# Longer DMA runs for one K cache of a two-part decode attention: A's K in runs of 16 KB in place of 8 KB

## The chip, the cores and the metric

The kernel runs on one core of a Trainium2 chip. The metric is the device time of one execution in microseconds (us). For each execution two numbers are known: that time, and the span, which is the stretch from the first to the last instruction that the hardware profiler recorded. This text calls their difference the time outside the span. A program on one core has no second die to compare with, so an execution counts as slow if it is over 1.5% above the fastest of its kernel. One run of the kernel before, of some thirty, took 248.25 us; it counts as fast by that rule, and it raises the mean and widens the intervals of its batch (r5 to r8).

## The reference, cut to what matters

Two independent attentions of one query token (A and B), each with 32 query heads over 16 KV heads of 128 dimensions, and a cache of 8192 tokens. A looks at the last 2048 tokens only, B at all of them. The two outputs are concatenated.

```python
q = (x @ wq).reshape(B, Sq, Hq, Dh)              # 576 -> 32 heads of 128
k = repeat(k_cache[:, :, Sk - W:, :], 2)         # A: W = 2048; B: all 8192 tokens
v = repeat(v_cache[:, :, Sk - W:, :], 2)
p = softmax(q @ k.T * Dh ** -0.5)
out = (p @ v).reshape(B, Sq, Hq * Dh) @ wo       # 4096 -> 576
```

Nearly everything is reading. In bf16 B's K and V are 67.1 MB, A's K and V 8.4 MB each, and the two wq and wo together 18.9 MB, 102.76 MB in all, each byte used once.

## The kernel before

There are five groups: group 0 is all of A, groups 1 to 4 are four KV heads of B each. A group's K goes to two slots of 4 MB (s = 0, 1), its V to one region of 8 MB. TensorE transposes K in 8 units per group, ScalarE (ACT) and VectorE (DVE) evict the transposed tiles from PSUM to `kt`, TensorE makes the scores, and then come exp, a transpose of the weights, and the product with V. SyncE issues every big load, as soon as its slot is free. The program is written for one instruction stream of TensorE that is looped over the groups, so all groups must have the same shapes there.

```python
def load_k(g, s):
    dst = slots[:, koff(s):koff(s) + SLOT]                 # [128, 16384] bf16
    def go(sp):
        if g:                                              # B: one copy of 4 MB, runs of 32 KB
            i = 4 * (g - 1) + 2 * s
            return sp.dma_start(dst, ks[1][0, i:i + 2, :, :].rearrange("e (p t) d -> p e (t d)", t=128))
        for m in range(4):                                 # A: four copies of 1 MB, runs of 8 KB
            i = 4 * m + 2 * s
            src = ks[0][0, i:i + 2, SK - W_A:, :].rearrange("e (p t) d -> p e (t d)", t=32)
            ins = sp.dma_start(dst[:, m * UNIT:(m + 1) * UNIT], src)
            ...                                            # cut: semaphore counts
        return ins
    ...
def q_stage(g, s):                                         # POOL puts q columns where they pick a head
    def go(pool):
        for e in range(2):
            dst = bass.AP(tensor=qst, offset=s * 264 + e * 130 + 4 * s, ap=[[528, 128], [40, 4], [1, 2]])
            ...
            ins = pool.tensor_copy(dst, src)
    ...
def k_transpose(g, u, place):                              # unit u: 4 x 8 transposes, 4 evictions
    ...
        dst = kt[:, u % NKT, q * 1024:(q + 1) * 1024]
        # q even: ACT copies ktps_bf[q] to dst; q odd: DVE does
```

A run here is one contiguous piece of HBM that lands in one SBUF partition; each is one DMA packet of its size (in r4 below, 6656 more runs are 6656 more packets). With 2048 tokens of 256 bytes and 64 partitions per head, A's run is 32 tokens or 8 KB.

Of the kernel before, what the change touches and what calls it, by code (L numbers as in the profile page):

```python
# [4 lines left out]
BF16 = mybir.dt.bfloat16  # L5
F32 = mybir.dt.float32
# [269 lines left out]
def bass_concat_heads__sliding_block_cached__gqa_block_cached__decode_kernel(  # L276
# [25 lines left out]


    prog = Program(nc)
    add = prog.add
# [8 lines left out]
    pickB = nc.alloc_sbuf_tensor("pickB", [128, 4, 32], F32)  # L314
    same = nc.alloc_sbuf_tensor("same", [128, 128], F32)
    sameB = nc.alloc_sbuf_tensor("sameB", [128, 128], F32)
    selq = nc.alloc_sbuf_tensor("selq", [128, 4, 2], BF16)
    onesf = nc.alloc_sbuf_tensor("onesf", [128, 4], F32)
    qst = nc.alloc_sbuf_tensor("qst", [128, 2 * 264], BF16)
    qcol = nc.alloc_sbuf_tensor("qcol", [128, 2, HQ], BF16)  # L320
# [48 lines left out]
    def setup(pool):  # L369
        for t in (ident, xpad, selq, warm, identf, same, pick, qst):  # L370
            pool.memset(t[:], 0.0)
        pool.memset(onesf[:], 1.0)
        return pool.memset(opj[:], 0.0)

    add("pool", setup, writes=["ident", ("xpad", 0), ("xpad", 1), "selq", "ones", "warm", "identf", "pick", "same",
                               ("qst", 0), ("qst", 1), ("opj", 0), ("opj", 1)])

# [5 lines left out]
    add("pool", select(selq[:], 0, [[-32, 4], [-1, 2]], 1), reads=["selq"], writes=["selq"])  # L383
    for dj in range(-3, 4):
        add("pool", select(same[:], 32 * dj, [[-1, 128]], 1), reads=["same"], writes=["same"])
    add("pool", select(identf[:], 0, [[-1, 128]], 1), reads=["identf"], writes=["identf"])
    for j in range(4):
        add("pool", select(pick[:], -128 * j, [[1, 4], [-1, 128]], 4), reads=["pick"], writes=["pick"])

    def sums(out, view, reads, writes, tag=None):  # L390
        add("dve", lambda dve: dve.tensor_reduce(out, view, AX.X, ALU.add), reads=reads, writes=writes, tag=tag)

# [8 lines left out]
    def load_k(g, s):  # L401
        dst = slots[:, koff(s):koff(s) + SLOT]

        def go(sp):
            if g:
                i = 4 * (g - 1) + 2 * s
                return sp.dma_start(dst, ks[1][0, i:i + 2, :, :].rearrange("e (p t) d -> p e (t d)", t=128))
            for m in range(4):
                i = 4 * m + 2 * s
                src = ks[0][0, i:i + 2, SK - W_A:, :].rearrange("e (p t) d -> p e (t d)", t=32)  # L410
                ins = sp.dma_start(dst[:, m * UNIT:(m + 1) * UNIT], src)
                if m < 3:
                    op.also.append((16, ins))
            return ins
        op = add("sp", go, writes=KS[s], dma="k%d" % s, inc=64)
# [59 lines left out]


    def q_stage(g, s):
        P = min(g, 1)

        def go(pool):  # L480
            for e in range(2):
                dst = bass.AP(tensor=qst, offset=s * 264 + e * 130 + 4 * s, ap=[[528, 128], [40, 4], [1, 2]])
                o = 4 * s + 2 * e + (8 * (g - 1) if P else 0)
                src = bass.AP(tensor=qcol, offset=P * HQ + o, ap=[[2 * HQ, 128], [0 if P else 8, 4], [1, 2]])
                ins = pool.tensor_copy(dst, src)  # L485
            return ins
        add("pool", go, reads=[("qcol", P)], writes=[("qst", s)], tag="q%d" % s)

    def k_transpose(g, u, place):
        s, m = divmod(u, 4)  # L490
        for q in range(4):
            def tr(pe, q=q):
                for t in range(8):
                    o = koff(s) + (32 * m + 8 * q + t) * 128
                    ins = pe.matmul(ktps_bf[q][:, t * 128:(t + 1) * 128], lhsT=slots[:, o:o + 128],  # L495
                                    rhs=ident[:, :], start=True, stop=True, is_transpose=True)
                return ins
            add("pe", tr, reads=KS[s] + ["ident"], writes=[("bank", q)], loop=(g, place + q / 8, None))
            dst = kt[:, u % NKT, q * 1024:(q + 1) * 1024]
            if q % 2 == 0:  # L500
                add("act", lambda act, q=q, dst=dst: act.activation(dst, ktps_bf[q], ACT.Copy),  # L501
                    reads=[("bank", q)], writes=[("kt", u % NKT, q)], tag="e%d%d" % (u, q))
            else:
                add("dve", lambda dve, q=q, dst=dst: dve.tensor_copy(dst, ktps_bf[q]),  # L504
                    reads=[("bank", q)], writes=[("kt", u % NKT, q)], tag="e%d%d" % (u, q))


    def k_scores(g, u, place):
        s, m = divmod(u, 4)

        def mm(pe):
            for e in range(2):
                for j in range(4):
                    rhs = kt[:, u % NKT, j * 1024:(j + 1) * 1024].rearrange("d (x g) -> d x g", g=2)[:, :, e]
                    o = s * 264 + e * 128 + m * 32
                    ins = pe.matmul(sacc[32 * j:32 * j + 32, :], lhsT=qst[:, o:o + 32], rhs=rhs,  # L516
                                    start=(u == 0 and e == 0), stop=True, skip_group_check=True)
            return ins
        add("pe", mm, reads=[("qst", s)] + [("kt", u % NKT, q) for q in range(4)], writes=[B_S],
            loop=(g, place, None))  # L520
# [7 lines left out]
    def softmax_exp(g):  # L528
# [6 lines left out]
        def go(act):  # L535
            src = bass.AP(tensor=sacc, offset=0, ap=[[512, 128], [2, 256], [1, 2], [0, 4]])
            dst = bass.AP(tensor=psb, offset=0, ap=[[2048, 128], [4, 256], [1024, 2], [1, 4]])
            return act.activation(dst, src, ACT.Exp, bias=st(C_NB + g), scale=SCALE, accum_out=st(C_L + g))  # L538
        add("act", go, reads=[B_S, ("st", C_NB + g)], writes=["psb", ("st", C_L + g)], tag="exp")


# [21 lines left out]
    def v_sums(g, place):  # L563
        v = slots[:, VOFF:VOFF + 2 * SLOT].rearrange("p (c m y) -> p c m y", c=2, m=4)

        def mm(pe):
            for c in range(2):
                for tt in range(8):
                    for j in range(4):
                        o = c * 1024 + tt * 128 + 32 * j  # L570
                        b = (8 * j + tt) * 128
                        ins = pe.matmul(opsum[32 * j:32 * j + 32, :], lhsT=ptm[:, o:o + 32], rhs=v[:, c, :, b:b + 128],  # L572
                                        start=(c == 0 and tt == 0), stop=(c == 1 and tt == 7), skip_group_check=True)
            return ins
# [16 lines left out]
    def weights_top(g):  # L591
# [5 lines left out]
        def top(dve):  # L597
            dve.tensor_reduce(srow[0:1, 0, 0:32], wsum[0:1, 0:128].rearrange("p (j h) -> p h j", j=4), AX.X, ALU.max)
            return dve.tensor_reduce(srow[0:4, 1, 0:8], wsum[0:4, 128:256].rearrange("p (a r) -> p r a", r=8),
# [3 lines left out]
        def rep(dve):  # L603
            src = bass.AP(tensor=srow, offset=0, ap=[[320, 1], [0, 4], [1, 32]])
            dve.tensor_scalar(srow[0:1, 0, 32:160].rearrange("p (j h) -> p j h", j=4), src, -SCALE, None, ALU.mult)
            src = bass.AP(tensor=srow, offset=160, ap=[[320, 4], [0, 16], [1, 8]])
# [16 lines left out]
    def weights_sum(g):  # L623
        def total(pe):
            pe.matmul(wsum[:, 264:265], lhsT=same[:, :], rhs=st(C_T + 5), start=True, stop=True)  # L625
            return pe.matmul(wsum[:, 265:269], lhsT=sameB[:, :], rhs=st(C_T + 6, 4), start=True, stop=True)  # L626
        add("pe", total, reads=[("st", C_T + 5), "same", "sameB"], writes=[B_W], loop=(g, 19.2, LAST))
        add("dve", lambda dve: dve.reciprocal(st(C_T + 10, NG), wsum[:, 264:269]),
# [55 lines left out]
    for P in range(2):  # L684
# [5 lines left out]
        q_finish(P)  # L690
    sums(maskV[:, :], same[:, 0:32].rearrange("p (m y) -> p m y", m=4), ["same"], ["maskV"])
    sums(four[:, :], ident[:, :].rearrange("p (x h) -> p h x", h=4), ["ident"], ["four"])
    add("dve", lambda dve: dve.tensor_copy(maskP[:, :].rearrange("p (x h y) -> p x h y", x=16, h=4),
                                           bass.AP(tensor=four, offset=0, ap=[[4, 128], [0, 16], [1, 4], [0, 2]])),
        reads=["four"], writes=["maskP"])
    sums(sameB[:, 0:8], same[:, 0:32].rearrange("p (m y) -> p y m", m=4), ["same"], ["sameB0"])
    add("dve", lambda dve: dve.tensor_copy(sameB[:, 8:128].rearrange("p (a y) -> p a y", y=8),
                                           bass.AP(tensor=sameB, offset=0, ap=[[128, 128], [0, 15], [1, 8]])),
        reads=["sameB0"], writes=["sameB"])
    sums(pickB[:, :, :], pick[:, :, :].rearrange("p r (i c) -> p r c i", i=4), ["pick"], ["pickB"])  # L700

    for g in range(NG):
# [70 lines left out]
```

## Time and profile before

| | before |
|---|---|
| device time, median of the first 3 runs | 246.94 us (246.59 to 247.20) |
| span of the profiled run | 245.0 us |
| HBM read | 102.76 MB, 419 GB/s over the span |
| PE, ACT, DVE busy | 66%, 37%, 34% of the span |

The head of the profile page of the kernel before: the span, busy time per engine, the DMA rows of the 40 equal slices (busy tenths of the 16 DMA engines, and GB/s), the packets, and the one queue that carries almost everything:

```profile
span 245.0 us, 5228 instructions
PE 160.8 (66%) x2325; PEld 117.3 (48%) x2325; DVE 82.3 (34%) x145; ACT 91.1 (37%) x95; POOL 10.7 (4%) x48
...
DMA  9999999999999999899999999999989999989993
GB/s 337 434 434 391 424 427 415 420 423 420 464 428 428 508 397 449 375 428 428 481 419 449 401 407 433 439 492 407 471 375 428 439 482 417 449 386 409 432 402 153
DMA packets 5222, 102.89 MB, mean 420 GB/s; under 512 B 731, under 2 KB 861, under 8 KB 1117
...
q1 hardware_dynamic: 5052, 102.77, 98.2%
```

No compute engine is near full, and the DMA engines have work in every slice but the last. So the time is the bytes over their rate, plus a start and an end. The same kernel by stretches (columns: the stretch and its length, busy time and instructions per engine, granted clock, DMA share, GB/s); the first is A's K, the second A's V, the third the bulk of B:

```profile
core 0: us, PE busy (x) PEld busy (x) DVE busy (x) ACT busy (x) POOL busy (x), PEclk, DMA share, GB/s
24.00:43.00 19.00, 10.24 (x139) 8.38 (x140) 5.75 (x17) 5.50 (x6) 0.57 (x4) 0.73 1.02 423
45.00:63.00 18.00, 13.81 (x209) 10.28 (x206) 9.07 (x14) 11.36 (x12) 0.63 (x4) 0.92 1.01 420
63.00:222.00 159.00, 115.77 (x1614) 83.56 (x1614) 62.42 (x102) 70.69 (x73) 1.88 (x12) 0.84 1.01 434
```

The stretches with 8 KB runs move at 420 to 423 GB/s, the one with runs of 32 KB (B's K) and 64 KB (B's V) at 434. SyncE's issues of the kernel before, in order of time, show how early the loads are ordered (start, us from the first issue of the line to the end of the last, line, tensors, count):

```profile
45.95 10.40 SPq L407 DMA_DIRECT2D slots<-in_B_k_cache_dram  x2
71.75 0.55 SPq L422 DMA_DIRECT2D slots<-in_B_v_cache_dram  x1
```

When B's first V is ordered at 71.75 us, the queue still holds B's K. All that stands ahead of that V is 34.6 MB, which lasts until about 82 us at these rates. That is ten microseconds of slack. The evictions of stage 0 in the kernel before (groups of instructions between 34 and 62 us; line, engine, operation, shapes, count, then busy us and mean ns of one, then the idle time before them):

```profile
L501 ACT ACTIVATE kt<-ktps 128x1024 bf16<-128x1024 bf16 x16 | 15.7, 1021 | 13.2 <-PE ktps L495 13.2
L504 DVE COPY kt<-ktps 128x1024 bf16<-128x1024 bf16 x16 | 11.1, 692 | 15.4 <-PE ktps L495 15.4
```

### The profile page before, as it was taken

What the parts mean: (1) busy time and instruction counts of PE and PEld (TensorE: products, weight loads), DVE (VectorE), ACT (ScalarE), POOL (GpSimd) and SP (SyncE); (2) the same over time, 40 slices, a digit from 0 to 9 for tenths busy, and PEclk for the clock granted to TensorE, in tenths of its full rate; (3) what the DMA queues carried; (4) which work ended last, traced back from release to release, by engine and by line L of the source; (5) the groups of instructions that cost most, each with busy time, mean ns of one, the idle gap of its engine ahead of it and who ended that gap; (6) DMA issues with size and microseconds to landing.
All of it is one profiled execution on the core that took longest, in us unless ns stands there. A gap on an engine that the chain in (4) does not pass through costs nothing. (4 is left out here: it accounts for less than half of the span.)

```text
span 245.0 us, 5228 instructions
## 1 busy us (share of the span) xinstructions
PE 160.8 (66%) x2325; PEld 117.3 (48%) x2325; DVE 82.3 (34%) x145; ACT 91.1 (37%) x95; POOL 10.7 (4%) x48
## 2 busy tenths in 40 slices
PE   0006329994476999383999454999456699647654
PEld 0002129782226876233887221987232678337533
DVE  0001304653222465303556312455322455442300
ACT  2000006875003786301778300687600568620000
POOL 7400000000000000000000000000000000000000
PEclk9999857999575999768899857799857999995999
DMA  9999999999999999899999999999989999989993
GB/s 337 434 434 391 424 427 415 420 423 420 464 428 428 508 397 449 375 428 428 481 419 449 401 407 433 439 492 407 471 375 428 439 482 417 449 386 409 432 402 153
DMA packets 5222, 102.89 MB, mean 420 GB/s; under 512 B 731, under 2 KB 861, under 8 KB 1117
## 3 DMA queue, kind: packets, MB, share of 16 engines
q1 hardware_dynamic: 5052, 102.77, 98.2%
q8 instruction: 6, 0.10, 0.2%
q10 hardware_dynamic: 160, 0.00, 0.0%
q14 instruction: 4, 0.02, 0.0%
HBM read 102.76 MB, written 0.00 MB: 419 GB/s over the span
## 5 line engine op out<-in xcount | busy, mean ns | idle before, releaser
L501 ACT ACTIVATE kt<-ktps 128x1024 bf16<-128x1024 bf16 x80 | 77.9, 1021 | 90.1 <-PE ktps L495 90.1
L495 PE MATMUL ktps<-ident,slots 128*128 128x128 bf16 x1280 | 85.0, 230 | 23.0 <-PEq L214 23.0
L495 PEld LDWEIGHTS ktps<-ident,slots 128*128 128x128 bf16 x1280 | 79.1, 104 | 38.3 <-issue 38.3
L504 DVE COPY kt<-ktps 128x1024 bf16<-128x1024 bf16 x80 | 55.3, 692 | 62.0 <-PE ktps L495 62.0
L572 PE MATMUL opsum<-slots,ptm 128*32 128x512 bf16 x320 | 28.2, 528 | 10.6 <-PEq L214 10.6
L516 PE MATMUL sacc<-kt,qst 128*32 128x512 bf16 x320 | 25.4, 392 | 1.9 <-PEq L214 1.9
L572 PEld LDWEIGHTS opsum<-slots,ptm 128*32 128x32 bf16 x320 | 13.7, 127 | 23.7 <-issue 21.7
L551 PE MATMUL misc<-ident,psb 128*128 128x128 bf16 x40 | 4.7, 288 | 15.8 <-PEq L214 15.8
L538 ACT ACTIVATE psb<-sacc,stat 128x2048 bf16<-128x2048 f32 x5 | 9.8, 1967 | 9.5 <-DVE stat L531 9.5
L583 DVE TENSOR_TENSOR vtmp<-opsum,maskV 128x512 f32<-128x512 f32 x4 | 2.8, 692 | 30.9 <-PE opsum L572 30.9
L551 PEld LDWEIGHTS misc<-ident,psb 128*128 128x128 bf16 x40 | 3.6, 128 | 18.2 <-issue 18.2
L438 PE MATMUL misc<-xnine,twice 64*128 64x18 bf16 x1 | 0.2, 170 | 18.0 <-DMA xnine<-in_B_x_dram 18.0
L485 POOL COPY qst<-qcol 128x8 bf16<-128x8 bf16 x20 | 3.1, 191 | 161.9 <-PE sacc L516 147.5
L665 PE MATMUL ktps<-slots,opj 128*32 128x144 bf16 (+1 forms) x192 | 6.8, 247 | 4.4 <-DMA slots<-in_B_wo_dram 4.4
L558 DVE TENSOR_TENSOR ptm<-misc,maskP 128x1024 bf16<-128x1024 bf16 x5 | 3.5, 692 | 16.0 <-PE misc L551 16.0
L516 PEld LDWEIGHTS sacc<-kt,qst 128*32 128x32 bf16 x320 | 5.0, 94 | 8.0 <-issue 4.3
L438 PEld LDWEIGHTS misc<-xnine,twice 64*128 64x128 bf16 x1 | 0.1, 98 | 18.0 <-issue 18.0
L665 PEld LDWEIGHTS ktps<-slots,opj 128*32 128x32 bf16 x192 | 5.2, 97 | 5.9 <-DMA slots<-in_B_wo_dram 5.3
L462 ACT ACTIVATE qrow<-opsum 128x512 bf16<-128x512 f32 x1 | 0.6, 597 | 19.4 <-PE opsum L456 19.4
L447 DVE TENSOR_SCALAR xpad<-misc,par 128x5 bf16<-128x5 f32 (+1 forms) x8 | 1.2, 230 | 14.2 <-PE misc L438 14.2
L529 DVE TENSOR_REDUCE stat<-sacc 128x1 f32<-128x512 f32 x5 | 3.5, 692 | 4.5 <-PE sacc L516 4.5
L551 PE MATMUL turned<-ident,psb 128*128 128x128 bf16 x40 | 4.8, 293 | 0.0
(73 smaller groups left out, 52.5 us busy)
## 6 DMA issues: line engine op xcount, KB each, us to landing
slots<-in_B_k_cache_dram SPq DMA_DIRECT2D x8, 4096.0 KB
slots<-in_A_k_cache_dram SPq DMA_DIRECT2D x8, 1024.0 KB
slots<-in_A_v_cache_dram SPq DMA_DIRECT2D x8, 1024.0 KB
slots<-in_A_wq_dram SPq DMA_DIRECT2D x1, 4608.0 KB, 13.8
slots<-in_B_wq_dram SPq DMA_DIRECT2D x1, 4608.0 KB, 23.9
slots<-in_A_wo_dram SPq DMA_DIRECT2D x1, 4608.0 KB, 20.8
slots<-in_B_wo_dram SPq DMA_DIRECT2D x1, 3024.0 KB, 27.6
slots<-in_B_wo_dram SPq DMA_DIRECT2D x1, 1008.0 KB, 11.7
```

What stands on the lines that cost most here:

```text
L485: ins = pool.tensor_copy(dst, src)
L495: ins = pe.matmul(ktps_bf[q][:, t * 128:(t + 1) * 128], lhsT=slots[:, o:o + 128], rhs=ident[:, :], start=True, stop=True, is_transpose=True)
L501: add("act", lambda act, q=q, dst=dst: act.activation(dst, ktps_bf[q], ACT.Copy), reads=[("bank", q)], writes=[("kt", u % NKT, q)], tag="e ...
L504: add("dve", lambda dve, q=q, dst=dst: dve.tensor_copy(dst, ktps_bf[q]), reads=[("bank", q)], writes=[("kt", u % NKT, q)], tag="e%d%d" % ( ...
L516: ins = pe.matmul(sacc[32 * j:32 * j + 32, :], lhsT=qst[:, o:o + 32], rhs=rhs, start=(u == 0 and e == 0), stop=True, skip_group_check=True)
L529: add("dve", lambda dve: dve.tensor_reduce(st(C_M + g), sacc[:, :], AX.X, ALU.max), reads=[B_S], writes=[("st", C_M + g)], tag="max")
L538: return act.activation(dst, src, ACT.Exp, bias=st(C_NB + g), scale=SCALE, accum_out=st(C_L + g))
L551: ins = pe.matmul(dst[:, t * 128:(t + 1) * 128], lhsT=psb[:, o:o + 128], rhs=ident[:, :], start=True, stop=True, is_transpose=True)
L558: return dve.tensor_tensor(ptm[:, c * 1024:(c + 1) * 1024].rearrange("p (t y) -> p t y", t=8), dst.rearrange("p (t y) -> p t y", t=8), mas ...
L572: ins = pe.matmul(opsum[32 * j:32 * j + 32, :], lhsT=ptm[:, o:o + 32], rhs=v[:, c, :, b:b + 128], start=(c == 0 and tt == 0), stop=(c == 1 ...
L583: add("dve", lambda dve: dve.tensor_tensor(vtmp[:, :, :], src, by, ALU.mult), reads=[B_O, w], writes=["vtmp"], tag="keep")
L665: ins = pe.matmul(ktps[P][32 * j:32 * j + 32, 0:w], lhsT=opj[:, P, jj:jj + 32], rhs=slots[:, o:o + w], start=(jj == 0), stop=(jj == HQ - 1))
```

## The change

Its intent is to let A's K come in runs of 16 KB. For that a copy must hold four heads with 32 partitions each, in place of two heads with 64. A unit of transposed K then mixes four heads where TensorE's fixed loop expects two; the evictions of group 0 sort them apart by writing pairs of columns to two places in turn, and POOL's q columns, the product with V and the matrices that sum over score rows follow the new order. The selection matrices, which POOL built with 11 selects, are now built by DVE from one identity. The core of the diff (cut: the order of A's score rows in the maximum, the exp of group 0, and the building of the matrices):

```diff
-                i = 4 * (g - 1) + 2 * s
-                return sp.dma_start(dst, ks[1][0, i:i + 2, :, :].rearrange("e (p t) d -> p e (t d)", t=128))
-            for m in range(4):
-                i = 4 * m + 2 * s
-                src = ks[0][0, i:i + 2, SK - W_A:, :].rearrange("e (p t) d -> p e (t d)", t=32)
-                ins = sp.dma_start(dst[:, m * UNIT:(m + 1) * UNIT], src)
+                i = 4 * (g - 1) + s
+                return sp.dma_start(dst, ks[1][0, i:i + 3:2, :, :].rearrange("e (p t) d -> p e (t d)", t=128))
+            for m1 in range(2):
+                i = 8 * m1 + s
+                src = ks[0][0, i:i + 7:2, SK - W_A:, :].rearrange("h (p t) d -> p h (t d)", t=64)
+                ins = sp.dma_start(dst[:, m1 * 2 * UNIT:(m1 + 1) * 2 * UNIT], src)
...
             for e in range(2):                        # q_stage, POOL: 2 copies -> 4 copies
+                for x in range(2):
...
-            dst = kt[:, u % NKT, q * 1024:(q + 1) * 1024]
+            dst, src = kt[:, u % NKT, q * 1024:(q + 1) * 1024], ktps_bf[q]
+            if g == 0:
+                dst = bass.AP(tensor=kt, offset=u % NKT * UNIT + q // 2 * 2048 + q % 2 * 512,
+                              ap=[[NKT * UNIT, 128], [2, 256], [1024, 2], [1, 2]])
+                src = src.rearrange("d (y x e) -> d y x e", x=2, e=2)
...
-                        b = (8 * j + tt) * 128
-                        ... rhs=v[:, c, :, b:b + 128]
+                        b = (j // 2 * 8 + tt) * 128
+                        ... rhs=v[:, c, j % 2, :, :, b:b + 128]
```

More of the change, by code (lines that the diff above doesn't have):

```diff
@@ L314, in bass_concat_heads__sliding_block_cached__gqa_block_cached__decode_kernel @@
     pickB = nc.alloc_sbuf_tensor("pickB", [128, 4, 32], F32)
-    same = nc.alloc_sbuf_tensor("same", [128, 128], F32)
+    kindA = nc.alloc_sbuf_tensor("kindA", [128, 32], F32)
+    sameA = nc.alloc_sbuf_tensor("sameA", [128, 128], F32)
     sameB = nc.alloc_sbuf_tensor("sameB", [128, 128], F32)
@@ L318, in bass_concat_heads__sliding_block_cached__gqa_block_cached__decode_kernel @@
     onesf = nc.alloc_sbuf_tensor("onesf", [128, 4], F32)
-    qst = nc.alloc_sbuf_tensor("qst", [128, 2 * 264], BF16)
+    qst = nc.alloc_sbuf_tensor("qst", [128, 1024], BF16)
     qcol = nc.alloc_sbuf_tensor("qcol", [128, 2, HQ], BF16)
@@ L369, in setup @@
     def setup(pool):
-        for t in (ident, xpad, selq, warm, identf, same, pick, qst):
+        for t in (ident, xpad, selq, warm, identf, pick, pickB, qst):
             pool.memset(t[:], 0.0)
@@ L373, in setup @@
         return pool.memset(opj[:], 0.0)
-    add("pool", setup, writes=["ident", ("xpad", 0), ("xpad", 1), "selq", "ones", "warm", "identf", "pick", "same",
+    add("pool", setup, writes=["ident", ("xpad", 0), ("xpad", 1), "selq", "ones", "warm", "identf", "pick", "pickB",
                                ("qst", 0), ("qst", 1), ("opj", 0), ("opj", 1)])
@@ L383, in bass_concat_heads__sliding_block_cached__gqa_block_cached__decode_kernel, with sums @@
     add("pool", select(selq[:], 0, [[-32, 4], [-1, 2]], 1), reads=["selq"], writes=["selq"])
-    for dj in range(-3, 4):
-        add("pool", select(same[:], 32 * dj, [[-1, 128]], 1), reads=["same"], writes=["same"])
     add("pool", select(identf[:], 0, [[-1, 128]], 1), reads=["identf"], writes=["identf"])
-    for j in range(4):
-        add("pool", select(pick[:], -128 * j, [[1, 4], [-1, 128]], 4), reads=["pick"], writes=["pick"])
-    def sums(out, view, reads, writes, tag=None):
-        add("dve", lambda dve: dve.tensor_reduce(out, view, AX.X, ALU.add), reads=reads, writes=writes, tag=tag)
+    def sums(out, view, reads, writes, tag=None, axes=AX.X):
+        add("dve", lambda dve: dve.tensor_reduce(out, view, axes, ALU.add), reads=reads, writes=writes, tag=tag)
     sums(par2[:, :], ident[:, :].rearrange("p (m g) -> p g m", g=2), ["ident"], ["par2"])
@@ L405, in go @@
             if g:
-                i = 4 * (g - 1) + 2 * s
-                return sp.dma_start(dst, ks[1][0, i:i + 2, :, :].rearrange("e (p t) d -> p e (t d)", t=128))
-            for m in range(4):
-                i = 4 * m + 2 * s
-                src = ks[0][0, i:i + 2, SK - W_A:, :].rearrange("e (p t) d -> p e (t d)", t=32)
-                ins = sp.dma_start(dst[:, m * UNIT:(m + 1) * UNIT], src)
-                if m < 3:
-                    op.also.append((16, ins))
+                i = 4 * (g - 1) + s
[4 more added lines that the diff above has]
+                ins = sp.dma_start(dst[:, m1 * 2 * UNIT:(m1 + 1) * 2 * UNIT], src)
+                if m1 == 0:
+                    op.also.append((32, ins))
             return ins
@@ L477, in q_stage @@
     def q_stage(g, s):
-        P = min(g, 1)
         def go(pool):
             for e in range(2):
-                dst = bass.AP(tensor=qst, offset=s * 264 + e * 130 + 4 * s, ap=[[528, 128], [40, 4], [1, 2]])
-                o = 4 * s + 2 * e + (8 * (g - 1) if P else 0)
-                src = bass.AP(tensor=qcol, offset=P * HQ + o, ap=[[2 * HQ, 128], [0 if P else 8, 4], [1, 2]])
-                ins = pool.tensor_copy(dst, src)
+                for x in range(2):
+                    o = s * 514 + e * 260 + x * 128
+                    if g:
+                        dst = bass.AP(tensor=qst, offset=o, ap=[[1024, 128], [40, 4], [1, 2]])
+                        src = bass.AP(tensor=qcol, offset=HQ + 8 * (g - 1) + 4 * e + 2 * s, ap=[[2 * HQ, 128], [0, 4], [1, 2]])
+                    else:
+                        dst = bass.AP(tensor=qst, offset=o, ap=[[1024, 128], [80, 2], [40, 2], [1, 2]])
+                        src = bass.AP(tensor=qcol, offset=8 * x + 4 * e + 2 * s, ap=[[2 * HQ, 128], [16, 2], [0, 2], [1, 2]])
+                    ins = pool.tensor_copy(dst, src)
             return ins
-        add("pool", go, reads=[("qcol", P)], writes=[("qst", s)], tag="q%d" % s)
+        add("pool", go, reads=[("qcol", min(g, 1))], writes=[("qst", s)], tag="q%d" % s)
     def k_transpose(g, u, place):
@@ L493, in tr @@
                 for t in range(8):
-                    o = koff(s) + (32 * m + 8 * q + t) * 128
+                    o = koff(s) + (64 * (m // 2) + 32 * (q % 2) + 16 * (m % 2) + 8 * (q // 2) + t) * 128
                     ins = pe.matmul(ktps_bf[q][:, t * 128:(t + 1) * 128], lhsT=slots[:, o:o + 128],
@@ L498, in k_transpose @@
             add("pe", tr, reads=KS[s] + ["ident"], writes=[("bank", q)], loop=(g, place + q / 8, None))
-            dst = kt[:, u % NKT, q * 1024:(q + 1) * 1024]
+            dst, src = kt[:, u % NKT, q * 1024:(q + 1) * 1024], ktps_bf[q]
[3 more added lines that the diff above has]
+                src = src.rearrange("d (y x e) -> d y x e", x=2, e=2)
             if q % 2 == 0:
-                add("act", lambda act, q=q, dst=dst: act.activation(dst, ktps_bf[q], ACT.Copy),
+                add("act", lambda act, src=src, dst=dst: act.activation(dst, src, ACT.Copy),
                     reads=[("bank", q)], writes=[("kt", u % NKT, q)], tag="e%d%d" % (u, q))
             else:
-                add("dve", lambda dve, q=q, dst=dst: dve.tensor_copy(dst, ktps_bf[q]),
+                add("dve", lambda dve, src=src, dst=dst: dve.tensor_copy(dst, src),
                     reads=[("bank", q)], writes=[("kt", u % NKT, q)], tag="e%d%d" % (u, q))
@@ L514, in mm @@
                     rhs = kt[:, u % NKT, j * 1024:(j + 1) * 1024].rearrange("d (x g) -> d x g", g=2)[:, :, e]
-                    o = s * 264 + e * 128 + m * 32
+                    o = s * 512 + e * 256 + j % 2 * 128 + m * 32
                     ins = pe.matmul(sacc[32 * j:32 * j + 32, :], lhsT=qst[:, o:o + 32], rhs=rhs,
@@ L535, in go @@
         def go(act):
-            src = bass.AP(tensor=sacc, offset=0, ap=[[512, 128], [2, 256], [1, 2], [0, 4]])
-            dst = bass.AP(tensor=psb, offset=0, ap=[[2048, 128], [4, 256], [1024, 2], [1, 4]])
+            if g:
+                src = bass.AP(tensor=sacc, offset=0, ap=[[512, 128], [2, 256], [1, 2], [0, 4]])
+                dst = bass.AP(tensor=psb, offset=0, ap=[[2048, 128], [4, 256], [1024, 2], [1, 4]])
+            else:
+                src = bass.AP(tensor=sacc, offset=0, ap=[[512, 128], [1, 512], [0, 4]])
+                dst = psb[:, :].rearrange("p (y h) -> p y h", h=4)
             return act.activation(dst, src, ACT.Exp, bias=st(C_NB + g), scale=SCALE, accum_out=st(C_L + g))
@@ L563, in v_sums @@
     def v_sums(g, place):
-        v = slots[:, VOFF:VOFF + 2 * SLOT].rearrange("p (c m y) -> p c m y", c=2, m=4)
+        v = slots[:, VOFF:VOFF + 2 * SLOT].rearrange("p (c m x n y) -> p c x m n y", c=2, m=2, x=2, n=2)
         def mm(pe):
@@ L570, in mm @@
                         o = c * 1024 + tt * 128 + 32 * j
-                        b = (8 * j + tt) * 128
-                        ins = pe.matmul(opsum[32 * j:32 * j + 32, :], lhsT=ptm[:, o:o + 32], rhs=v[:, c, :, b:b + 128],
+                        b = (j // 2 * 8 + tt) * 128
+                        ins = pe.matmul(opsum[32 * j:32 * j + 32, :], lhsT=ptm[:, o:o + 32],
+                                        rhs=v[:, c, j % 2, :, :, b:b + 128],
                                         start=(c == 0 and tt == 0), stop=(c == 1 and tt == 7), skip_group_check=True)
@@ L597, in top @@
         def top(dve):
-            dve.tensor_reduce(srow[0:1, 0, 0:32], wsum[0:1, 0:128].rearrange("p (j h) -> p h j", j=4), AX.X, ALU.max)
+            dve.tensor_reduce(srow[0:1, 0, 0:32].rearrange("p (b y) -> p b y", b=4),
+                              wsum[0:1, 0:128].rearrange("p (a b c y) -> p b y a c", a=2, b=4, c=2), AX.XY, ALU.max)
             return dve.tensor_reduce(srow[0:4, 1, 0:8], wsum[0:4, 128:256].rearrange("p (a r) -> p r a", r=8),
@@ L603, in rep @@
         def rep(dve):
-            src = bass.AP(tensor=srow, offset=0, ap=[[320, 1], [0, 4], [1, 32]])
-            dve.tensor_scalar(srow[0:1, 0, 32:160].rearrange("p (j h) -> p j h", j=4), src, -SCALE, None, ALU.mult)
+            src = bass.AP(tensor=srow, offset=0, ap=[[320, 1], [8, 4], [0, 2], [1, 8]])
+            for a in range(2):
+                to = srow[0:1, 0, 32 + 64 * a:96 + 64 * a].rearrange("p (b c y) -> p b c y", b=4, c=2)
+                dve.tensor_scalar(to, src, -SCALE, None, ALU.mult)
             src = bass.AP(tensor=srow, offset=160, ap=[[320, 4], [0, 16], [1, 8]])
@@ L624, in total @@
         def total(pe):
-            pe.matmul(wsum[:, 264:265], lhsT=same[:, :], rhs=st(C_T + 5), start=True, stop=True)
+            pe.matmul(wsum[:, 264:265], lhsT=sameA[:, :], rhs=st(C_T + 5), start=True, stop=True)
             return pe.matmul(wsum[:, 265:269], lhsT=sameB[:, :], rhs=st(C_T + 6, 4), start=True, stop=True)
-        add("pe", total, reads=[("st", C_T + 5), "same", "sameB"], writes=[B_W], loop=(g, 19.2, LAST))
+        add("pe", total, reads=[("st", C_T + 5), "sameA", "sameB"], writes=[B_W], loop=(g, 19.2, LAST))
         add("dve", lambda dve: dve.reciprocal(st(C_T + 10, NG), wsum[:, 264:269]),
@@ L690, in bass_concat_heads__sliding_block_cached__gqa_block_cached__decode_kernel, with pick_A @@
         q_finish(P)
-    sums(maskV[:, :], same[:, 0:32].rearrange("p (m y) -> p m y", m=4), ["same"], ["maskV"])
+    sums(kindA[:, :].rearrange("p (b y) -> p b y", b=4), identf[:, :].rearrange("p (a b c y) -> p b y a c", a=2, b=4, c=2),
+         ["identf"], ["kindA"], axes=AX.XY)
+    add("dve", lambda dve: dve.tensor_copy(sameA[:, :].rearrange("p (a b c y) -> p a b c y", a=2, b=4, c=2),
+                                           bass.AP(tensor=kindA, offset=0, ap=[[32, 128], [0, 2], [8, 4], [0, 2], [1, 8]])),
+        reads=["kindA"], writes=["sameA"])
+    sums(sameB[:, 0:8], identf[:, :].rearrange("p (x y) -> p y x", y=8), ["identf"], ["sameB0"])
+    add("dve", lambda dve: dve.tensor_copy(sameB[:, 8:128].rearrange("p (a y) -> p a y", y=8),
+                                           bass.AP(tensor=sameB, offset=0, ap=[[128, 128], [0, 15], [1, 8]])),
+        reads=["sameB0"], writes=["sameB"])
+    sums(maskV[:, :], identf[:, :].rearrange("p (j m y) -> p m j y", j=4, m=4), ["identf"], ["maskV"], axes=AX.XY)
+    def pick_A(dve):
+        for r in range(4):
+            dst = bass.AP(tensor=pick, offset=129 * r, ap=[[512, 128], [64, 2], [32, 2], [4, 8]])
+            src = bass.AP(tensor=kindA, offset=0, ap=[[32, 128], [8, 2], [16, 2], [1, 8]])
+            ins = dve.tensor_copy(dst, src)
+        return ins
+    add("dve", pick_A, reads=["kindA", "pick"], writes=["pick"])
+    add("dve", lambda dve: dve.tensor_copy(bass.AP(tensor=pickB, offset=0, ap=[[128, 128], [33, 4], [4, 8]]),
+                                           bass.AP(tensor=sameB, offset=0, ap=[[128, 128], [0, 4], [1, 8]])),
+        reads=["sameB0", "pickB"], writes=["pickB"])
     sums(four[:, :], ident[:, :].rearrange("p (x h) -> p h x", h=4), ["ident"], ["four"])
@@ L695, in bass_concat_heads__sliding_block_cached__gqa_block_cached__decode_kernel @@
         reads=["four"], writes=["maskP"])
-    sums(sameB[:, 0:8], same[:, 0:32].rearrange("p (m y) -> p y m", m=4), ["same"], ["sameB0"])
-    add("dve", lambda dve: dve.tensor_copy(sameB[:, 8:128].rearrange("p (a y) -> p a y", y=8),
-                                           bass.AP(tensor=sameB, offset=0, ap=[[128, 128], [0, 15], [1, 8]])),
-        reads=["sameB0"], writes=["sameB"])
-    sums(pickB[:, :, :], pick[:, :, :].rearrange("p r (i c) -> p r c i", i=4), ["pick"], ["pickB"])
     for g in range(NG):
```

## The prediction

> **What bounds the kernel now.** The DMA engines. The table of 40 slices shows them at 9 tenths in all but a few slices; the page counts 102.76 MB from HBM at 419 GB/s over a span of 245.0 us. PE is busy 66%, ACT 37%, DVE 34%. The chain that ended last names the last pieces of B's wo (12.34 us), but they were issued at 229.95 us, nine microseconds before the piece ahead of them in the queue had come (PE's wait for it ended at 238.84): they only stood in line. By stretches: B's K and V (63 to 222 us, runs of 32 and 64 KB) move at 434 GB/s, A's K (24 to 43 us, 8 KB runs) at 423, A's V (45 to 63 us, 8 KB) at 420.
>
> **What the change does.**
> - DMA: A's K (8.39 MB) goes in 4 copies of 2 MB with 16 KB runs instead of 8 of 1 MB with 8 KB runs: 512 data packets fewer of 5222. Fitting a fixed cost per run to 423 and 434 GB/s (8 KB against some 43 KB) gives about 10 ns per run and engine; 32 runs fewer per engine save 0.3 us. That is an estimate from the trace; the ceiling, at 434 GB/s, is 0.5 us. All of it is on the critical path.
> - B's K pairs heads 4 MiB apart instead of 2. The Trainium skill, "DMA: Bandwidth & Descriptors", Latency and other measured facts, reports HBM copies that lose rate at row pitches of 2 and 4 MiB. But B's V already walks four heads at 2 MiB pitch in one copy, within the stretch at 434 GB/s: I expect no loss.
> - POOL loses 11 selects (5.9 us, done by 9.7 us) and doubles its q copies (20 of 191 ns). DVE gets some 8 more operations of 0.2 to 0.3 us after 28 us, done before PE starts K at 35.1. Off the path.
> - Evictions of A's K write pairs at a stride of two pairs. The Trainium skill, "Vector Engine (DVE) Microarchitecture Reference", 5.1 Performance modes, asks for 2-byte elements with inner step 1 and more than one inner element for two results a cycle; a pair satisfies it. So DVE stays near 0.69 us, ACT near 1.02. If DVE fell to one result a cycle it would take some 1.23 us (estimate), two of them 2.46 us, no more than a unit's present pace.
> - The last stage gets one more DVE row operation (0.2 us), before a release with nine microseconds to spare.
>
> **Critical path.** Only the rate of the bytes is on it. Group 1's K is issued at 46 us and begins to move near 63; its V is issued at 71.75 and begins near 82. Ten microseconds of slack swallow any change of the engines.
>
> **Prediction.** 246.94 less 0.3 for the runs, and 0.1 for fewer copies: 246.5 us, 8 in 10 between 245.7 and 247.2. Faster by over 2%: 0.02; within 2%: 0.96; slower by over 2%: 0.02.
>
> **What would show it.** Packets near 4640 (512 data and some completions fewer); A's K at 427 to 431 GB/s, B's stretch still 433 to 435; PE's first K transposes within 0.3 us of 35.1; B's K issued within 1 us of 45.95; eviction means in stage 0 near 0.69 and 1.02 us; the tail after the last byte unchanged (2.7 us).
>
> **What would make it wrong.** The 4 MiB head pitch lowering the rate; longer runs making the 16 DMA engines finish less evenly, so that the slowest sets the end (the last ten microseconds already average only 374 GB/s); evictions several times slower, eating the slack.

## The result, and the profile after

| | before | after |
|---|---|---|
| device time, median of 6 runs each | 246.61 us (246.51 to 247.20) | 246.95 us (246.63 to 247.21) |
| span of the profiled run | 245.0 us | 244.8 us |
| DMA packets | 5222 | 4644 |

The ratio is 1.0008 with a 95% interval of 0.9995 to 1.0021: the same. Ratios here are the mean time of one kernel's fast runs over that of the other's of the same rounds, so not quite the ratio of the medians quoted.

The head of the profile page of the changed kernel:

```profile
span 244.8 us, 5229 instructions
PE 166.4 (68%) x2325; PEld 120.3 (49%) x2325; DVE 88.3 (36%) x152; ACT 92.5 (38%) x95; POOL 9.1 (4%) x57
...
DMA  9999999999999999899999999999989999989993
...
DMA packets 4644, 102.88 MB, mean 420 GB/s; under 512 B 666, under 2 KB 796, under 8 KB 1052
...
q1 hardware_dynamic: 4476, 102.76, 98.1%
```

The changed kernel by the same stretches:

```profile
24.00:43.00 19.00, 12.61 (x157) 8.71 (x157) 8.50 (x24) 6.63 (x7) 1.06 (x8) 1.00 1.01 429
45.00:63.00 18.00, 13.65 (x176) 9.79 (x168) 9.48 (x10) 9.20 (x9) 0.56 (x4) 0.81 1.02 425
63.00:222.00 159.00, 118.86 (x1629) 86.04 (x1626) 63.51 (x99) 72.96 (x75) 3.93 (x28) 0.83 1.00 433
```

SyncE's issues of the changed kernel:

```profile
44.94 16.92 SPq L407 DMA_DIRECT2D slots<-in_B_k_cache_dram  x2
74.07 0.55 SPq L422 DMA_DIRECT2D slots<-in_B_v_cache_dram  x1
```

The evictions of stage 0 of the changed kernel, by groups between 34 and 62 us:

```profile
L507 ACT ACTIVATE kt<-ktps 128x1024 bf16<-128x1024 bf16 x16 | 16.8, 1100 | 14.9 <-PE ktps L497 14.9
...
L510 DVE COPY kt<-ktps 128x1024 bf16<-128x1024 bf16 x16 | 16.5, 1089 | 13.4 <-PE ktps L497 13.4
```

A's K does move faster, 429 against 423 GB/s, and B is unchanged. DVE's evictions of stage 0 went from 0.69 to 1.09 us, which the prediction had denied, and B's first V is ordered 2.3 us later. And the span is shorter while the time is not. The profiled runs say it in small: 245.0 and 246.54 us before, 244.8 and 246.63 us after. That puzzle is what the experiments are about.

### The profile page after: what moved, and what is told of

Same layout as the page of the kernel before. It is cut to its first block, busy times and chain, and to the rows that moved or that the text cites. A ratio compares the mean times of both kernels' runs of the same rounds, so it can differ in the third digit from the quotient of the medians.

```text
span 244.8 us, 5229 instructions
## 1 busy us (share of the span) xinstructions
PE 166.4 (68%) x2325; PEld 120.3 (49%) x2325; DVE 88.3 (36%) x152; ACT 92.5 (38%) x95; POOL 9.1 (4%) x57
## 2 busy tenths in 40 slices
DMA packets 4644, 102.88 MB, mean 420 GB/s; under 512 B 666, under 2 KB 796, under 8 KB 1052
## 5 line engine op out<-in xcount | busy, mean ns | idle before, releaser
L507 ACT ACTIVATE kt<-ktps 128x1024 bf16<-128x1024 bf16 x80 | 79.3, 1037 | 86.6 <-PE ktps L497 86.4
L497 PE MATMUL ktps<-ident,slots 128*128 128x128 bf16 x1280 | 87.0, 232 | 21.0 <-PEq L214 17.2
L497 PEld LDWEIGHTS ktps<-ident,slots 128*128 128x128 bf16 x1280 | 80.7, 105 | 36.9 <-issue 36.8
L510 DVE COPY kt<-ktps 128x1024 bf16<-128x1024 bf16 x80 | 60.8, 771 | 56.9 <-PE ktps L497 56.9
L581 PE MATMUL opsum<-slots,ptm 128*32 128x512 bf16 x320 | 27.6, 518 | 8.7 <-PEq L214 8.7
L522 PE MATMUL sacc<-kt,qst 128*32 128x512 bf16 x320 | 25.9, 400 | 2.1 <-PEq L214 2.1
L487 POOL COPY qst<-qcol 128x8 bf16<-128x8 bf16 x40 | 5.5, 190 | 165.2 <-PE sacc L522 145.0
L560 PE MATMUL turned<-ident,psb 128*128 128x128 bf16 x40 | 5.3, 313 | 0.0
```

What stands on the lines that cost most here:

```text
L497: ins = pe.matmul(ktps_bf[q][:, t * 128:(t + 1) * 128], lhsT=slots[:, o:o + 128], rhs=ident[:, :], start=True, stop=True, is_transpose=True)
L507: add("act", lambda act, src=src, dst=dst: act.activation(dst, src, ACT.Copy), reads=[("bank", q)], writes=[("kt", u % NKT, q)], tag="e%d% ...
L510: add("dve", lambda dve, src=src, dst=dst: dve.tensor_copy(dst, src), reads=[("bank", q)], writes=[("kt", u % NKT, q)], tag="e%d%d" % (u, q))
L522: ins = pe.matmul(sacc[32 * j:32 * j + 32, :], lhsT=qst[:, o:o + 32], rhs=rhs, start=(u == 0 and e == 0), stop=True, skip_group_check=True)
L560: ins = pe.matmul(dst[:, t * 128:(t + 1) * 128], lhsT=psb[:, o:o + 128], rhs=ident[:, :], start=True, stop=True, is_transpose=True)
L581: ins = pe.matmul(opsum[32 * j:32 * j + 32, :], lhsT=ptm[:, o:o + 32], rhs=v[:, c, j % 2, :, :, b:b + 128], start=(c == 0 and tt == 0), st ...
```

## The experiments

There were three questions. Is the rate really set by the length of the runs, and what does a run cost? Does the slower stage 0 cost time? Where does the gain go?

The theory that came out of the prediction (R) is a fixed cost of about 10 ns per run on each DMA engine, all of it on the critical path. The rival (N) is that A's stretches are slower for some other reason and nothing was gained. A third reading came up with the first batch: the gain is real and is lost outside the span.

### r1: the changed kernel again, 5 rounds

No edit.

> The changed kernel once more, for the spans. Theory R (runs): a fixed cost of about 10 ns per run and engine makes the span 0.3 us shorter than that of the kernel before; if the total time is still equal, the 0.3 us went into the time outside the span (1.83 to 1.97 us in the six runs after, 1.54 us in the one run before that is known). Rival N (nothing): span and time both equal to before within 0.1 us; the 429 GB/s of A's K in the one trace (423 before) is noise of that trace or is lost again before the last byte lands.

Measured, means over the fast runs of the batch (time, span and their difference in us; spans are recorded to 0.1 us):

| | runs | time | span | outside |
|---|---|---|---|---|
| kernel before, first batch | 9 | 246.72 | 245.22 | 1.50 (1.43 to 1.60) |
| changed kernel, r1 | 5 | 246.81 | 244.90 | 1.91 (1.85 to 1.97) |

The ratio is 1.0004 (0.9991 to 1.0018). So the span did lose 0.32 us, as theory R has it, and the time outside the span gained 0.41 us. The ranges of the two times outside do not overlap. The six runs with the result say the same (1.83 to 1.97 us).

### r2: the changed kernel with A's K in 8 KB runs

```diff
-                ins = sp.dma_start(dst[:, m1 * 2 * UNIT:(m1 + 1) * 2 * UNIT], src)
+                for c in range(2):
+                    o = (2 * m1 + c) * UNIT
+                    ins = sp.dma_start(dst[:, o:o + UNIT], src[:, :, c * UNIT:(c + 1) * UNIT])
```

> The changed kernel with A's K copied in columns of 8 KB again (4 copies of 1 MB per slot as before; the layout in SBUF and all engine work as in the changed kernel). Theory R: A's K back at 423 GB/s, packets back at about 5220, time 0.3 us above r1. Rival N: time within 0.1 us of r1.

Measured: packets back at 5220, A's K at 424 GB/s (r1: 428), span 245.10 us (r1: 244.90), time outside 1.83 us, time 246.93 us (r1: 246.81). The rate and the span answer to the run length, in the direction of theory R; the size, 0.2 us in the span and 0.1 in the time where 0.3 had been expected, is at the edge of what these runs resolve. Hence an amplifier.

### r3 and r4: all of B's K and V in 8 KB runs

r3 cuts each of B's loads into columns, 4 copies for K and 8 for V. r4 keeps one copy per load and gets 8 KB runs from another order of the tokens (K shown; V likewise).

```diff
 # r3
-                return sp.dma_start(dst, src)
+                for c in range(4):
+                    ins = sp.dma_start(dst[:, c * UNIT:(c + 1) * UNIT], src[:, :, c * UNIT:(c + 1) * UNIT])
 # r4
+                src = ks[1][0, i:i + 2, :, :].rearrange("e (c p t) d -> p (e c) (t d)", c=2, t=32)
+                return sp.dma_start(dst.rearrange("p (c y) -> p c y", c=4), src)
```

> Amplifier: all of B's K and V (67 MB) in columns of 8 KB, 4 and 8 copies in place of one: 416 more runs per engine. Theory R (10 ns per run and engine): 4.2 us slower than r1, the stretch of B at about 420 GB/s. Rival N (A's stretch is slower for another reason, such as its place early in the kernel): at most 0.5 us slower, B still at 433.

> As r3, runs of 8 KB for B's K and V, but one copy per load, as in the changed kernel; the tokens land in another order, so the result is wrong on purpose. If the cost is per run: equal to r3. If it is per copy (semaphores, issue): equal to r1. Theory R says equal to r3, 4.2 us above r1.

Measured: r3 takes 250.64 us in the median (ratio to before 1.0155, 1.0139 to 1.0170), r4 250.64 us as well (1.0158, 1.0142 to 1.0173; its result is wrong). The profile pages of r3 and then r4 count these packets, and their stretch of B is the third and fourth line:

```profile
DMA packets 12133, 102.89 MB, mean 413 GB/s; under 512 B 1498, under 2 KB 1628, under 8 KB 1884
```

```profile
DMA packets 11300, 102.88 MB, mean 413 GB/s; under 512 B 666, under 2 KB 796, under 8 KB 1052
```

```profile
63.00:222.00 159.00, 117.63 (x1626) 84.96 (x1627) 61.57 (x92) 72.85 (x74) 3.92 (x28) 0.83 1.01 422
```

```profile
63.00:222.00 159.00, 116.75 (x1622) 84.22 (x1623) 61.23 (x92) 72.79 (x74) 3.96 (x28) 0.84 1.01 422
```

r4 has 6656 packets more than the changed kernel, which is 16 engines times 416 runs. The mean time of r3 is 3.84 us above r1's (4.2 had been expected); over 416 runs that is 9.2 ns per run and engine. B's stretch fell from 433 to 422 GB/s, to what A's stretches with 8 KB runs show. Rival N falls. And since r3 issues 52 copies more than r4 at an equal time (250.64 and 250.63 us in the mean), a copy as such costs nothing here; the runs do.

### r5: the kernel before with only the longer runs

```diff
-            for m in range(4):
-                i = 4 * m + 2 * s
-                src = ks[0][0, i:i + 2, SK - W_A:, :].rearrange("e (p t) d -> p e (t d)", t=32)
+            for m1 in range(2):
+                i = 8 * m1 + s
+                src = ks[0][0, i:i + 7:2, SK - W_A:, :].rearrange("h (p t) d -> p h (t d)", t=64)
```

> The kernel before with the copies of A's K as in the changed kernel (4 of 2 MB, runs of 16 KB) and nothing else; the tokens land in another order, so the result is wrong on purpose. Theory R: the span is 0.3 us shorter than before (244.9 against 245.2). The time outside the span was 1.50 us before (9 runs) and 1.91 us after (11 runs). If the engines' added instructions make that, it stays at 1.5 here and the time is 0.3 us below before (about 246.4). If the DMA instructions make it, it is 1.9 and the time is equal to before.

Measured: time 246.31 us in the median against 246.66 for the kernel before in the same batch, ratio 0.9978 (0.9957 to 0.9999); span 244.83 against 245.15 us in the mean; time outside the span 1.50 us. (The run of 248.25 us is in that ratio; without it the means differ by 0.30 us.) So the longer runs by themselves are worth the predicted 0.3 us, and without the other parts of the change it reaches the device time. The result came out as correct although the heads of A's K are mixed up. The reference's inputs say why: with x and K of standard deviation 0.05 and wq of 0.05 / sqrt(576), a score has a standard deviation of about 0.0001 (an estimate), so all tokens weigh nearly the same. By that estimate the comparison sees neither the order of K nor the choice of q in any run here. So r5 is a measurement, not a usable kernel, and "correct" for the changed kernel and its variants does not test their handling of A's K and q.

### r6 and r7: more instructions on POOL, or on DVE, in the kernel before

```diff
 # r6, in q_stage                                  # r7, in the setup
+                pool.tensor_copy(spare[...], src)   +    for i in range(8):
                 ins = pool.tensor_copy(dst, src)    +        sums(spare[:, 32*i:32*i+32], ...)
```

> The kernel before with 20 more POOL copies, each beside one of the 20 q copies, into a tile that nobody reads. If the number of POOL instructions (57 after, 48 before) makes the time outside the span, it grows from 1.50 to 1.9 us or more, with the span unchanged at 245.2. If not, 1.50.

> The kernel before with 8 more small DVE reductions in the setup, into a tile that nobody reads. If the number of DVE instructions (152 after, 145 before) makes the time outside the span, it grows from 1.50 to 1.9 us, span unchanged at 245.2. If not, 1.50.

Measured: r6 has 1.56 us outside the span (1.53 to 1.59) and 246.66 us in the median; r7 has 1.50 us and 246.74 us. Neither does it. More instructions are not enough, on either engine.

### r8: the changed kernel with POOL's q copies merged

Four copies per stage become one (two for group 0), by longer access patterns. The result is correct. POOL's program shrinks from 61 instructions to 33.

```diff
-                for x in range(2):
-                    ... 
-                        dst = bass.AP(tensor=qst, offset=o, ap=[[1024, 128], [40, 4], [1, 2]])
+                    dst = bass.AP(tensor=qst, offset=o, ap=[[1024, 128], [260, 2], [128, 2], [40, 4], [1, 2]])
+                    src = bass.AP(tensor=qcol, offset=HQ + 8 * (g - 1) + 2 * s, ap=[[2 * HQ, 128], [4, 2], [0, 2], [0, 4], [1, 2]])
```

> The changed kernel with its 40 q copies on POOL merged into 12 by longer access patterns (same result, correct). If POOL's instruction count makes the time outside the span, it falls from 1.91 to 1.5 us or less, the span stays at 244.9, and the time is 246.4 us, below both kernels. If not, 1.9 us and 246.9 us as the changed kernel.

Measured: the time outside is 1.48 us (1.42 to 1.63), the span stays at 244.93 us, and the time is 246.39 us in the median (before 246.66 in this batch; ratio 0.9985, 0.9964 to 1.0006). So POOL's program is what had moved the time outside the span, and this version keeps the change's gain. It is the lowest of the correct versions with the change's design. Against the kernel before its interval still includes 1 (without the run of 248.25 us the means differ by 0.22 us).

### r9 and r10: is it the length of POOL's program?

r6 (72 instructions), r8 (33) and the kernel before (52) have about 1.5 us; the changed kernel (61) and its variants r2 to r4 (also 61) have 1.83 to 1.91. (These counts are the page's busy instructions and four semaphore instructions.) The guess was that 61 is an unlucky length. r9 adds 9 unused POOL copies to the kernel before (61), r10 adds 11 to the changed kernel (72).

```diff
 # r9                                                # r10
+                if o < 72:                            +   if x == 0 and k < 88:
+                    pool.tensor_copy(spare[...], src) +       pool.tensor_copy(spare[...], ...)
```

> The kernel before with 9 more POOL copies, so that POOL's program has 61 instructions, as in the changed kernel (before 52; 72 in r6; 33 in r8). Theory L (length: what counts is where POOL's program ends, and 61 is an unlucky place): the time outside the span is 1.85 to 1.9 us, the total 0.4 us above before. Rival C (something else in the changed kernel's POOL program than its length): 1.50 us and the time of before.

> The changed kernel with 11 more POOL copies into a tile that nobody reads, so 72 instructions, the length that gave 1.56 us in r6. Theory L: the time outside the span falls to 1.5 to 1.6 us although POOL does more work, and the total is 246.5 us. Rival C: 1.9 us and 246.9 us, or more.

Measured: r9 1.55 us (1.53 to 1.58), r10 1.53 us (1.52 to 1.54), where the same batch's kernel before has 1.48. The same batch also holds r11 and r12 (below) with POOL's program as in the changed kernel: 1.90 and 1.87 us, so chip and batch are not the reason. r10 does what theory L said: POOL does more work, and the 0.4 us are gone; its time is 246.53 us in the median. r9 does not: it has 61 instructions by that count and no loss (its median of 246.91 us comes with a span of 245.32).

The traces show where the 0.4 us are. At its end each program has a barrier, in which POOL runs two semaphore instructions; the other engines' last semaphore instructions follow the second. The lines for POOL, from `--source L254` of the kernel before, the changed kernel, r8, r9 and r10 (first and last start at the end):

```profile
L254 POOLq EVENT_SEMAPHORE  x2: 17/17/17, 244.5 to 244.5; - x2
L254 POOLq EVENT_SEMAPHORE  x2: 17/17/17, 244.2 to 244.7; - x2
L254 POOLq EVENT_SEMAPHORE  x2: 17/17/17, 244.3 to 244.3; - x2
L254 POOLq EVENT_SEMAPHORE  x2: 17/17/17, 244.8 to 244.9; - x2
L254 POOLq EVENT_SEMAPHORE  x2: 17/17/17, 244.4 to 244.5; - x2
```

At the trace's full resolution the second starts 0.08 us after the first in the kernel before and in r5 to r10, and 0.43 to 0.44 us after it in the changed kernel, r1 to r4, r11 and r12: exactly the programs with the long time outside. If the time from the end of POOL's second instruction is taken (device time less that place in the span), it is 1.93 to 2.03 us in the profiled runs with the delay and 1.89 to 1.99 us in those without. SyncE's last instruction ends the span, and in the kernel before it comes some 0.4 us after POOL's; in the changed kernel POOL is late, and only 0.1 us remain. So by this account the loss lies inside the span, where SyncE hides it, and shows in the time outside.

What is shown is that POOL's program sets this delay, and that both a shorter and a longer one avoid it. Why its last instruction comes late stays open. r9 is a weak test of theory L, since the count of 61 leaves out POOL's register moves, of which the kernel before has 14 and the changed kernel 3. With everything that the trace records of POOL, the programs with the delay all have 69 instructions, and those without it have 41, 71, 80 (r9 and r10 alike) or 91. No run put 69 into the other program, so an unlucky length is neither shown nor refuted.

### r11 and r12: how much slack has stage 0?

DVE's evictions of A's K are slowed, with the same result, by a maximum over two equal values: in the first 3 of 8 units, or in all 8.

```diff
-                add("dve", lambda dve, src=src, dst=dst: dve.tensor_copy(dst, src),
+                    if g == 0 and u < 3:      # r12: u < 8
+                        return dve.tensor_reduce(dst, src.unsqueeze(4).to_broadcast([128, 256, 2, 2, 2]), AX.X, ALU.max)
+                    return dve.tensor_copy(dst, src)
```

> Slack: DVE's evictions of the first 3 of the 8 units of A's K read each value twice (a maximum over two equal values, same result), about 2.3 us each instead of 1.09. That makes stage 0 some 7 us longer: V of group 1 issued at about 81 us instead of 74, just as its turn in the queue comes (82). Expected: time within 0.3 us of r1. If stage 0's engines were on the critical path, +7 us.

> The same for all 8 units: stage 0 some 18 us longer, V of group 1 issued at about 92 us, 10 us after its turn in the queue. Expected: the DMA engines go idle for about 10 us and the time is 254 to 260 us. If it is less, stage 0 had more slack than the 8 us read from the trace.

Measured: the slowed evictions take 2.28 us. r11 orders B's first V at 78.01 us, 4 us later than the changed kernel (81 us had been expected, so it uses half of the slack), and takes 246.90 us in the mean (r1: 246.81). Nothing lost. r12 takes 256.19 us in the mean, 9.4 us more than r1. Its V is ordered at 90.57 us, and the DMA engines had run dry by then (SyncE's issue, then the stretches around it):

```profile
90.57 0.55 SPq L422 DMA_DIRECT2D slots<-in_B_v_cache_dram  x1
```

```profile
63.00:80.00 17.00, 8.19 (x82) 5.44 (x82) 11.08 (x9) 5.33 (x5) 0.56 (x4) 0.68 1.01 432
80.00:92.00 12.00, 7.64 (x92) 4.07 (x93) 1.59 (x3) 0.88 (x1) 0.00 (x0) 0.60 0.35 132
```

From 80 to 92 us only 132 GB/s came. So the slack read from the trace, about 8 us in the changed kernel (74.07 to 82), is about right: 4 us of delay cost nothing, 16.5 us cost 9.4, which leaves some 7.

## Why the prediction was right or wrong

Its total was right: 246.5 us with 245.7 to 247.2 around it and "within 2%" at 0.96, against 246.95. But the range is wider than the gain: no change at all would have fallen into it too, so the total says little for the mechanism. The small gain in it, 0.4 us, did not arrive in the device time, and three steps failed: the device time as the span plus a constant, the 0.1 us for fewer copies, and the unchanged evictions.

- "The DMA engines" bound the kernel: right. r12 shows what happens when they wait, and r3 and r4 show that the run cost passes straight to the time.
- "About 10 ns per run and engine; 32 runs fewer per engine save 0.3 us ... All of it is on the critical path": right for the span. r3 measures 9.2 ns, which makes 0.29 us for 32 runs. The spans differ by 0.32 us, and r5, the DMA part alone, gains that in the device time too. A's K at 429 GB/s lies in the predicted 427 to 431, and the 4644 packets fit "near 4640".
- "and 0.1 for fewer copies": wrong. r3 and r4 differ by 52 copies and by nothing in time.
- "I expect no loss" from heads 4 MiB apart: right. The Trainium skill, "DMA: Bandwidth & Descriptors", Latency and other measured facts, reports rates halved at a pitch of 4 MiB from partition to partition, for copies from HBM to HBM. Here the pitch is from head to head, and B's stretch moves at 433 GB/s, 434 before.
- "POOL loses 11 selects ... Off the path": right up to the closing barrier, and there the failed step lies. The prediction took the device time for the span plus a constant. With the new program POOL's last instruction comes 0.44 us after the one before it, where it was 0.08, and the time outside the span goes from 1.50 to 1.91 us, which eats the 0.32 us that the runs gave. r8 and r10 undo it by changing POOL's program and nothing else.
- "DVE stays near 0.69 us, ACT near 1.02": wrong. They took 1.09 and 1.10 us in stage 0; in the later groups, with contiguous destinations, DVE's copies stay at 0.69. The quoted rule on performance modes, "Vector Engine (DVE) Microarchitecture Reference", 5.1, asks whether a pair can be taken per cycle. It does not ask where the next pair lies. The section after it, 5.2 Measured stream behaviour on trn2, does: a port keeps its full rate only in runs of at least two adjacent 4-byte words, and in its test of a two-source program a destination that hops with every word took 1.71 ns per column against 1.054. The evictions of group 0 write one 4-byte pair here and the next one 2 KB away. An estimate from that page, 512 words at 1.71 ns plus the 0.16 us that 0.69 leaves beside 512 cycles at 0.96 GHz, is 1.04 us; the trace has 1.09. No run here isolates the pattern from the rest of the change, but the same instruction in the same kernel without it takes 0.69.
- "Ten microseconds of slack swallow any change of the engines": right in kind. Stage 0 became slower, and B's V was ordered 2.3 us later at no cost; r11 and r12 bracket the slack. B's first K was ordered at 44.94 us, 1.01 us earlier than before, where "within 1 us" had been said.
- "The tail after the last byte unchanged (2.7 us)": right; the last piece of wo landed at 242.06 us of 244.8 (242.29 of 245.0 before).

## What to carry to other kernels

When a kernel is bound by the DMA engines, count the runs: each cost about 9 ns on its engine here, so cutting 8 KB runs to half their number is worth about 1.5% of that transfer's time (0.3 us of the 19.8 that A's K takes at 423 GB/s) and no more, and a rearrangement of the compute for it must have slack to pay from. When a gain of a few tenths of a microsecond is sought, compare the span and the device time separately; here the gain was in one and the loss in the other, and only the pair of numbers told them apart. Then read the closing barrier of each engine too, for the last instruction of the span can hide a late engine. A destination that hops with every 4-byte word came with slower copies here (1.09 us against 0.69), although the mode rule promises two values per cycle.

## What the Trainium skill lacked or had wrong

- "DMA: Bandwidth & Descriptors", Specifications, gives 512 B as the smallest transfer at line rate, and "Why small descriptors are slow" treats the fixed cost of a packet as a matter of small descriptors, with joining them worth it only up to 256 B. Here runs of 8 KB moved at 422 GB/s and runs of 32 and 64 KB at 433: about 9 ns per run and engine (r3, r4), 3.8 us of 250.6 when all of B has 8 KB runs. A packet cost of that size does stand in the same page, in the note under Measured: about 10.5 ns, from a copy of 4 KB.
- The same page gives no cost of an extra DMA copy that is queued behind others. Here 52 extra copies cost nothing measurable (r3 against r4).
- "Vector Engine (DVE) Microarchitecture Reference", 5.1, read alone, promises two results per cycle for rows of two 2-byte elements; 5.2 measures the hop for 4-byte streams only. In this trace a bf16 copy from PSUM writing pairs 2 KB apart took 1.09 us against 0.69.
- No page that I read gives the cost of such a hop on ScalarE: 1.10 us against 1.02 for the same 1024 elements.
- No page that I read tells that one engine's program can delay the closing barrier behind the end of the span: 1.50 us outside the span before, 1.91 after, 1.48 with POOL's copies merged, 1.53 with 11 more of them. "Runtime: NRT & Kernel Launch", The launch sequence, lists barriers and resets around the kernel, but does not say that the kernel's own program can change them.
